# Two linear layers behind a state attention, one core: leaky ReLU on ScalarE, conversion paced by VectorE's time, turned state reads, earlier loads in the tail

## The chip, the core and the metric

The kernel runs on one core of one Trainium2 chip. Its engines have queues of their own and wait for each other by semaphores: TensorE (PE, with a queue PEld for weight loads), VectorE (DVE), ScalarE (ACT), GpSimd (POOL), and SyncE (SP), which here issues nearly all DMAs. The metric is the device time of one execution in microseconds.

## What is computed

```python
def _attn_ref(x, state):                  # x: 8 x 8 x 512 x 64, state: 8 x 8 x 32 x 64
    scores = scale * np.matmul(x, state.transpose(0, 1, 3, 2))
    ...                                   # softmax over the 32 states
    xread = np.matmul(a, state)
    scores2 = scale * np.matmul(state, x.transpose(0, 1, 3, 2))
    ...                                   # softmax over the 512 tokens
    sread = np.matmul(a2, x)
    return np.concatenate([xread, sread], axis=2)

def _moe_ref(x, w_in, w_out):             # 4352 x 512 -> 2048 -> 512
    h = x @ w_in
    g = np.maximum(0.01 * h, h)
    return g @ w_out

def _moe2_ref(x, w_gate, w_val, w_out):   # 512 -> 1536 -> 512
    g = x @ w_gate
    silu = g * (1.0 / (1.0 + np.exp(-g)))
    return silu * (x @ w_val) @ w_out
```

The weights come as 64-bit floats and are rounded to 32 bits by the kernel itself.

## The kernel before

**Numbers as high and low parts.** A product of two 32-bit matrices is made of three matmuls (`passes`): each operand is split into a high part, a cast on ACT (`split_h`, L162), and a low part, a subtraction on DVE (`split_l`, L165). Matmuls of the split parts move up to 512 columns each.

**Layer 1.** There are eight blocks of 512 tokens and, as a ninth, the tail: the 256 rows that the state reads make. `N1` = 128 slots run in one loop, 16 for each block; a slot `i` takes one of the 16 groups of 128 hidden columns. In it, `h_mm` makes the hidden values of the slot two ahead (6 matmuls into `ps_h`), `h_act` applies the leaky ReLU (an ACT copy from PSUM, L515, and a DVE operation, L516) and splits the result into `gh` and `gl`, and `y_mm` adds the slot's share to the block's output (12 matmuls into `ps_y`). In the last block (slots 112 to 127) each slot also does the tail's share (`h_mm(B, ...)`, `y_mm(B, ...)`, 256 columns, with weights `tail_in` that are split into `ch` and `cl`). The attention's steps (`read_state`, `read_tokens`) are put into slots beforehand by `put`, which keeps the sum of their DVE costs in a slot under `BUDGET`. `read_tokens` ends in `read` (16 products of 128x32 weights `et` and 64 moving columns `xn`, L400) and `read_out` (8 transposes of 32x32 from PSUM on DVE, L413).

**The conversion in the background.** Layer 2's weights have to be rounded and split before layer 2 can start. `convert` is a generator over 36 pieces ("keys") of w_gate, w_val and w_out: each key is loaded from DRAM into one of three buffers `ws`, and takes two operations on ACT (`scale`, `low`) and four on DVE (`limit` L216, `sign` L213, `join` L219, `add` L222). `finish2` is a second generator that takes finished keys in pairs, makes sums and splits of them (`hl`) and stores them in DRAM (`quad_...`, `w2_...`, `wo_...`). `pump(n)` advances the first by n steps, `pump_finish(n)` the second; a key's work is four steps. In blocks 1 to 6 a slot calls `pump(1)` once, and once more in each fourth slot; the same holds for `pump_finish`. In the last block's slots there are seven `pump(1)` and a `pump_finish(5)`. In slot `Y_SUMS` = 6 of the last block, whatever is left of both generators is run down on the spot (the drain); then its memory is handed over to the pool `wpool`, 16 places for layer 2's weights, and the first of these are loaded (`load_w`, `wq`), as are the inputs (`yr`) of `y_sums`, sums and splits of finished blocks that layer 2 starts from (`yc`, `T`).

**Order.** The program text sets the order on each engine (`manual_schedule`): an instruction that waits holds up all that stand behind it on its engine. SP issues DMAs in text order as well, with at most eight under way.

**Layer 2** goes over four pairs of blocks: products by `quads` (`ps_x`, `ps_s`, `ps_a`; L708), then `read_out(p)`, 24 steps of 12 matmuls with w_out (`ps_o`, `wo`). A step's end frees a place for the `wo` load four steps on (`load_wo`, L806). Before the last pair comes the tail: twelve steps `f`, each `hidden(f)` (24 matmuls of 256 columns into `ps_t`, with split gate and val weights `wh`, `wl`) and 6 matmuls into `ps_o`. The tail's first six generator steps run between the steps of `read_out(2)`: the first loads, the splits of `y`, and the splits of gate and val for `f` = 0 and 1. `split2` splits a loaded weight `wraw` and calls `load2` for the next load in the fixed order gate, val, o of f = 0, 1, 2 and so on. Three loads are made ahead.

Of the kernel before, what the change touches and what calls it, by code (L numbers as in the profile page):

```python
# [25 lines left out]
def kernel(  # L26
# [38 lines left out]
    nc = tc.nc  # L65
# [47 lines left out]
    Y_SUMS = 6  # L113
# [4 lines left out]
    PUMPS = [1, 1, 1, 1, 1, 1, 1]  # L118
    BUDGET = 2.8
    EARLY = -5  # L120
    BUDGET0 = 2.6
# [39 lines left out]
    def split_h(dst, src):  # L161
        nc.scalar.copy(dst, src)  # L162
# [68 lines left out]
    def convert(keys, room, prepare, load_next, finish=None):  # L231

        done, before, prev = None, None, None
        for key in keys + [None, None]:
            while key and not room(key):
                yield 0
            ops = None
# [9 lines left out]
            yield 1  # L247
# [3 lines left out]
            yield 1  # L251
            if prev:
                prev["join"]()
            yield 1
# [9 lines left out]
            yield 1  # L264
# [9 lines left out]
    def pump_finish(n):  # L274
        for _ in range(n):
            next(finishing[0], None)
# [84 lines left out]
    def read_tokens(b, q):  # L361
# [32 lines left out]
        def read():  # L394

            ps = v["ps"] = ps_a.tile([P, 512], F32, tag="b", name="ps_r")
            tokens = [xn.pop((b, p)) for p in pairs]
            for c in range(NC):
                for j in range(4):
                    nc.tensor.matmul(  # L400
                        ps[NS * j:NS * (j + 1), 0:D],
                        lhsT=v["et"][:, c * P + NS * j:c * P + NS * (j + 1)],
                        rhs=tokens[j // 2][:, c, D * (j % 2):D * (j % 2 + 1)],
                        start=(c == 0),
                        stop=(c == NC - 1),
                    )
            next_xn(2)

        def read_out():
            for j in range(4):  # L410
                for g in range(2):
                    d0 = D * (j % 2) + 32 * g
                    nc.vector.transpose(  # L413
                        out=x_tail[d0:d0 + 32, pairs[j // 2], b * NS:(b + 1) * NS],
                        in_=v["ps"][NS * j:NS * (j + 1), 32 * g:32 * g + 32],
                    )
# [6 lines left out]
            {"D": [read_out], "cost": 0.9},  # L423
# [82 lines left out]
    def h_act(j, f):  # L506
# [8 lines left out]
        nc.scalar.copy(hs, ps[:, :n])  # L515
        nc.vector.scalar_tensor_tensor(out=hs, in0=hs, scalar=0.01, in1=hs, op0=ALU.mult, op1=ALU.max)  # L516
# [174 lines left out]
    def layer2(p2, ps2):  # L691
# [167 lines left out]
        def tail():  # L859
            n = widths[B]  # L860
            order = [(key, f) for f in range(NF2) for key in ("gate", "val", "o")]
            loads = iter(order)
            raw2, parts2 = {}, {}

            def load2():
                key = next(loads, None)
                if not key:
                    return
                kind, f = key
                if kind == "o":  # L870
# [5 lines left out]
                    parts2[key] = (h, l), (ht, lt)  # L876
                else:
                    raw2[key] = wtiles[0].take("wraw")
                    nc.sync.dma_start(out=raw2[key][0], in_=w2_dram[kind, f % HF][:, f // HF])
# [7 lines left out]
            for _ in range(3):  # L887
                load2()
# [11 lines left out]
            def split2(kind, f):  # L900
                if f < NF2:
                    if kind != "o":
                        t, tag = raw2.pop((kind, f))
                        h, ht = wtiles[0].take("wh", dtype=F32R)
                        l, lt = wtiles[0].take("wl", dtype=F32R)
                        split_h(h, t)
                        split_l(l, t, h)
                        wtiles[0].give(tag)
                        parts2[kind, f] = (h, l), (ht, lt)
                    load2()  # L910
# [27 lines left out]
            split2("o", 0)  # L938
            yield
            hidden(0)  # L940
            for f in range(NF2):
                split2("gate", f + 2)
                split2("val", f + 2)
                split2("o", f + 1)
# [12 lines left out]
                wtiles[0].give(*tags)  # L957
                if f + 2 >= NF2:
# [494 lines left out]
```

## Time and profile before

| | |
|---|---|
| median of 3 runs | 1517.83 us (1517.43 to 1518.1) |
| profiled execution | 1516.83 us |
| its span, first to last instruction | 1515.0 us |
| PE busy | 1460.5 us, 96% |
| DVE busy | 944.6 us, 62% |
| ACT busy | 683.4 us, 45% |
| mean granted clock of TensorE | 0.984 |

The windows give busy times of each engine in a stretch of the span; the timeline gives single instructions with the idle time ahead of them and what ended it; the chain of waits is followed back from the last instruction. The granted clock of 1.00 is TensorE's upper level, 2.4 GHz, and 0.50 its lower one, 1.2 GHz; a mean between them is a stretch with both. Durations of matmuls are longer than the distance of their starts, because they are pipelined, so distances are used here.

### The profile page before, as it was taken

Reading aid. Unit: us, or ns where it says so; the run is one execution under the profiler, and the core shown is the slowest. Engines: PE = TensorE matmul, PEld = TensorE weight load, DVE = VectorE, ACT = ScalarE, POOL = GpSimd, SP = SyncE. Lnnn points to the kernel's source line nnn. Section 1 sums busy time; section 2 is a strip of 40 time slices with the busy share of each in tenths; the row PEclk is TensorE's granted clock in tenths of the full one; section 3 lists DMA queues with packets and bytes.
Section 4 is the critical chain, followed back from the end, with each engine's and each line's share of the span. In section 5 each row is a group of like instructions: output and inputs, shape, how many; then the busy total and the mean of one; then the engine's idle time right before and its main releaser. Section 6 shows DMA issues by size and latency. Waiting matters only on the chain.

```text
span 1515.0 us, 20085 instructions
## 1 busy us (share of the span) xinstructions
PE 1460.5 (96%) x7114; PEld 1157.6 (76%) x7114; DVE 944.6 (62%) x1716; ACT 683.4 (45%) x1234; POOL 3.0 (0%) x8
## 2 busy tenths in 40 slices
PE   6999999999999999919999999999999998999999
PEld 2446777777777788818888888888888887988887
DVE  6888688887887876976444544445344554544442
ACT  6777555565555555645433333334333342433322
POOL 0000000000000000000000000000000000000000
PEclk9999999999999999959999999999999998999999
DMA  8885444444454545785568677676766387786445
GB/s 296 294 282 198 140 157 177 153 174 157 164 194 161 188 137 183 262 271 183 162 193 274 205 235 229 194 221 228 235 200 194 105 285 230 225 279 192 130 141 193
DMA packets 146164, 307.53 MB, mean 203 GB/s; under 512 B 14608, under 2 KB 35088, under 8 KB 145040
## 3 DMA queue, kind: packets, MB, share of 16 engines
q1 hardware_dynamic: 144912, 297.85, 60.1%
q10 hardware_dynamic: 1152, 8.39, 1.3%
q8 instruction: 57, 0.93, 0.3%
q14 instruction: 43, 0.35, 0.1%
HBM read 231.74 MB, written 74.45 MB: 202 GB/s over the span
## 4 chain that ended last, share of the span: by engine, by line
PE 51%; DMA 4%; DVE 3%; ACT 1%; issue 0%; SPq 0%; ACTq 0%; DVEq 0%
PE ps_x L708 17%; PE ps_o L433 17%; PE ps_s L708 9%; PE ps_a L708 4%; DMA wraw<-w_val 2%; PE ps_y L433 1%; PE ps_h L433 1%; DMA ws<-in_dram 1%; PE ps_yt L433 1%; DMA wo<-wo 1%; PE ps_t L433 0%; DVE wl L165 0%; ACT wh L162 0%; DVE two L219 0%; DVE hl L165 0%
## 5 line engine op out<-in xcount | busy, mean ns | idle before, releaser
L433 PE MATMUL ps_y<-gh,w_parts 128*128 128x512 f32 x1024 | 339.0, 391 | 0.0
L708 PE MATMUL ps_x<-yc,wq 128*128 128x512 f32 x1152 | 278.0, 389 | 0.0
L708 PEld LDWEIGHTS ps_x<-yc,wq 128*128 128x128 f32 x1152 | 216.2, 188 | 44.8
L433 PE MATMUL ps_o<-wo,zh 128*128 128x512 f32 x768 | 236.5, 389 | 0.0
L433 PEld LDWEIGHTS ps_y<-gh,w_parts 128*128 128x128 f32 x1024 | 192.4, 188 | 52.0 <-issue 8.1
L433 PE MATMUL ps_y<-gl,w_parts 128*128 128x512 f32 x512 | 199.5, 390 | 0.2 <-DVE gl L165 0.2
L433 PEld LDWEIGHTS ps_o<-wo,zh 128*128 128x128 f32 x768 | 144.2, 188 | 30.0
L433 PE MATMUL ps_o<-wo,zl 128*128 128x512 f32 x384 | 149.5, 389 | 0.5 <-DMA wo<-wo 0.5
L708 PE MATMUL ps_s<-yc,wq 128*128 128x512 f32 x576 | 146.1, 389 | 0.0
L162 ACT CAST gh<-hs 128x512 fp32r<-128x512 f32 (+1 forms) x144 | 85.9, 596 | 118.1 <-DVE hs L516 118.1
L165 DVE TENSOR_TENSOR zl<-z,zh 128x512 fp32r<-128x512 f32 x96 | 66.3, 691 | 116.0 <-ACT zh L162 116.0
L165 DVE TENSOR_TENSOR gl<-hs,gh 128x512 fp32r<-128x512 f32 (+1 forms) x144 | 95.3, 662 | 56.9 <-ACT gh L162 54.0
L708 PEld LDWEIGHTS ps_s<-yc,wq 128*128 128x128 f32 x576 | 108.1, 188 | 22.4
L162 ACT CAST zh<-z 128x512 fp32r<-128x512 f32 x96 | 59.3, 622 | 142.1 <-PE ps_o L433 142.0
L728 ACT ACTIVATE sg<-C 128x512 f32<-128x512 f32 x72 | 45.5, 632 | 158.5 <-DVE C L724 158.5
L433 PEld LDWEIGHTS ps_y<-gl,w_parts 128*128 128x128 f32 x512 | 96.2, 188 | 20.1 <-DVE gl L165 0.5
L724 DVE TENSOR_TENSOR C<-ps_s,C 128x512 f32<-128x512 f32 x48 | 33.2, 691 | 124.2 <-PE ps_s L708 124.2
L516 DVE SCALAR_TENSOR_TENSOR hs<-hs 128x512 f32<-128x512 f32 (+1 forms) x144 | 94.5, 656 | 25.9 <-ACT hs L515 24.8
L515 ACT COPY hs<-ps_h 128x512 f32<-128x512 f32 (+1 forms) x144 | 80.5, 559 | 60.3 <-PE ps_h L433 58.5
L433 PE MATMUL ps_h<-ah,swl 128*128 128x512 f32 x256 | 106.4, 416 | 0.5 <-DVE swl L165 0.5
L433 PE MATMUL ps_h<-al,swh 128*128 128x512 f32 x256 | 100.6, 393 | 0.0
L433 PE MATMUL ps_h<-ah,swh 128*128 128x512 f32 x256 | 100.4, 392 | 0.0
(126 smaller groups left out, 2009.3 us busy)
## 6 DMA issues: line engine op xcount, KB each, us to landing
wo<-wo SPq DMA_DIRECT2D x96, 512.0 KB, 4.7
wq<-quad_gate SPq DMA_DIRECT2D x168, 256.0 KB, 3.1
wq<-quad_val SPq DMA_DIRECT2D x168, 256.0 KB, 3.1
ws<-in_dram SPq DMA_DIRECT2D x68, 512.0 KB, 4.6
sw_dram<-sw SPq DMA_DIRECT2D x56, 256.0 KB, 3.1
sw<-sw_dram SPq DMA_DIRECT2D x56, 256.0 KB, 3.8
quad_gate<-hl SPq DMA_DIRECT2D x24, 512.0 KB, 3.5
quad_val<-hl SPq DMA_DIRECT2D x24, 512.0 KB, 3.4
```

The costliest lines, as they stand in the source:

```text
L162: nc.scalar.copy(dst, src)
L165: nc.vector.tensor_tensor(out=dst, in0=src, in1=hi.bitcast(F32), op=ALU.subtract)
L433: nc.tensor.matmul(ps, lhsT=w, rhs=v, start=first and n == 0, stop=last and n == len(todo) - 1)
L515: nc.scalar.copy(hs, ps[:, :n])
L516: nc.vector.scalar_tensor_tensor(out=hs, in0=hs, scalar=0.01, in1=hs, op0=ALU.mult, op1=ALU.max)
L708: nc.tensor.matmul(bank, lhsT=a, rhs=v, start=first and n == 0, stop=last and n == len(todo) - 1, skip_group_check=True,)
L724: nc.vector.tensor_tensor(out=kept[0], in0=bank, in1=kept[0], op=ALU.add)
L728: nc.scalar.activation(t[0], c, AF.Sigmoid)
```

## The change

- The leaky ReLU is one ACT activation (Prelu) from PSUM instead of an ACT copy and a DVE operation.
- The generators' steps yield a cost in us of DVE's time. `fill(us)` runs both until the given time is used up. In blocks 1 to 6 a slot is given what is left of `SLOT` after `CHUNK` and the attention's steps, at most `FILL`, half of it ahead of `y_mm` and half behind. `pump` remains for block 0.
- In the last block each slot ahead of `Y_SUMS`, now 5, gets `fill(2.0)`. The sums' steps then run at a bounded pace, with the rest behind the loop.
- A state read is turned: `xn` (128x64) are the weights, 32 columns of `et` move, two products at a time lie in PSUM side by side, and one DVE copy takes the place of 8 transposes. Its cost for `put` is 0.2 instead of 0.9.
- In the tail's first step gate and val of f = 0 and 1 are loaded and both parts of w_out for both (8 loads instead of 4), and later loads are made two steps ahead.

```diff
-    Y_SUMS = 6
+    Y_SUMS = 5
...
-    PUMPS = [1, 1, 1, 1, 1, 1, 1]
+    BUDGET0 = 2.6
+    FILL = 1.9
+    CHUNK = 0.8
+    SLOT = 4.1
...
             if prev:
                 prev["limit"]()
-            yield 1
+            yield 0.42
             if key:
                 ops["low"]()
                 ops["sign"]()
-            yield 1
+            yield 0.42
             if prev:
                 prev["join"]()
-            yield 1
+            yield 0.69
...
-    def pump_finish(n):
-        for _ in range(n):
-            next(finishing[0], None)
+    credit = [0.0]
+
+    def fill(us):
+
+        credit[0] = min(credit[0] + us, 2.0)
+        while credit[0] > 0:
+            cost = (next(finishing[0], None) or 0) + (next(background[0], None) or 0)
+            if not cost:
+                break
+            credit[0] -= cost
...
-            ps = v["ps"] = ps_a.tile([P, 512], F32, tag="b", name="ps_r")
+            ps = v["ps"] = ps_a.tile([P, 2, NS], F32, tag="b", name="ps_r")
             tokens = [xn.pop((b, p)) for p in pairs]
-            for c in range(NC):
-                for j in range(4):
-                    nc.tensor.matmul(
-                        ps[NS * j:NS * (j + 1), 0:D],
-                        lhsT=v["et"][:, c * P + NS * j:c * P + NS * (j + 1)],
-                        rhs=tokens[j // 2][:, c, D * (j % 2):D * (j % 2 + 1)],
...
+            for i in range(2):
+                for c in range(NC):
+                    for e in range(2):
+                        n = c * P + NS * (2 * i + e)
+                        nc.tensor.matmul(
+                            ps[D * e:D * (e + 1), i],
+                            lhsT=tokens[i][:, c, D * e:D * (e + 1)],
+                            rhs=v["et"][:, n:n + NS],
...
+            nc.vector.tensor_copy(out=x_tail[:, pairs[0]:pairs[0] + 2, b * NS:(b + 1) * NS], in_=v["ps"])
...
-        nc.scalar.copy(hs, ps[:, :n])
-        nc.vector.scalar_tensor_tensor(out=hs, in0=hs, scalar=0.01, in1=hs, op0=ALU.mult, op1=ALU.max)
+        nc.scalar.activation(hs, ps[:, :n], AF.Prelu, alpha=0.01)
...
-            for _ in range(3):
-                load2()
+            for f in range(2):
+                for kind in ("gate", "val"):
+                    load2(kind, f)
+            for f in range(2):
+                load2("o", f)
...
+                    load2(kind, f + 2)
...
                 wtiles[0].give(*tags)
+                load2("o", f + 2)
...
-                pump(PUMPS[0])
+                room = min(FILL, SLOT - CHUNK - load.get(i, 0))
+                fill(room / 2)
                 next(parts)
-                pump_finish(1)
                 y_mm(j, f)
-                pump(f % 4 == 2)
-                pump_finish(f % 4 == 0)
+                fill(room / 2)
...
                 if f < Y_SUMS:
-                    pump_finish(5)
+                    fill(2.0)
                 elif f == Y_SUMS:
-                    while next(background[0], None) is not None or next(finishing[0], None) is not None:
-                        pump(1)
-                        pump_finish(1)
+                    drain()
...
-                    for _ in range(2):
+
+                    while summed[0] < min(2 * (f - Y_SUMS), f):
                         next(sums0, None)
+                        summed[0] += 1
```

DVE's queue in the last block, at the slot of the drain; a row is a line, an operation, and what it writes and reads (`two<-ws,two` as ISA is a key's `add`). Before:

```order
L165 TENSOR_TENSOR gl<-hs,gh 128x512
L213 TENSOR_SCALAR two<-ws 128x512
L219 SCALAR_TENSOR_TENSOR two<-ws,two 128x512
L222 ISA two<-ws,two 128x1024
L165 TENSOR_TENSOR hl<-two,hl 128x512 x2
L216 TENSOR_SCALAR ws<-ws 128x512
L213 TENSOR_SCALAR two<-ws 128x512
L219 SCALAR_TENSOR_TENSOR two<-ws,two 128x512
L222 ISA two<-ws,two 128x1024
```

Now, around the same slot and the one after it:

```order
L168 TENSOR_TENSOR gl<-hs,gh 128x256
L168 TENSOR_TENSOR gl<-hs,gh 128x512
L168 TENSOR_TENSOR cl<-tail_in,ch 128x512
L168 TENSOR_TENSOR gl<-hs,gh 128x256
L168 TENSOR_TENSOR gl<-hs,gh 128x512
L168 TENSOR_TENSOR swl<-sw,swh 128x512
L168 TENSOR_TENSOR cl<-tail_in,ch 128x512
L168 TENSOR_TENSOR gl<-hs,gh 128x256
L168 TENSOR_TENSOR gl<-hs,gh 128x512
L623 TENSOR_TENSOR T<-yr 128x512
```

Before, ten `add` stand between this `gl` and the next `cl`; now the 36th and last `add` stands behind 112 `gl`, ahead of the rows shown.

SP's queue in `read_out(2)`, where the tail's first loads stand between the `wo` loads. Before:

```order
L806 DMA wo<-wo_136 128x1024
L884 DMA yr<-y_dram_103 128x512 x2
L879 DMA wraw<-w_gate_108 128x512
L879 DMA wraw<-w_val_114 128x512
L875 DMA wh<-wo_132 128x512
L875 DMA wl<-wo_132 128x512
L806 DMA wo<-wo_133 128x1024
```

Now:

```order
L815 DMA wo<-wo_136 128x1024
L889 DMA yr<-y_dram_103 128x512 x2
L884 DMA wraw<-w_gate_108 128x512
L884 DMA wraw<-w_val_114 128x512
L884 DMA wraw<-w_gate_109 128x512
L884 DMA wraw<-w_val_115 128x512
L880 DMA wh<-wo_132 128x512
L880 DMA wl<-wo_132 128x512
L880 DMA wh<-wo_132 128x512
L880 DMA wl<-wo_132 128x512
L815 DMA wo<-wo_133 128x1024
```

Four more loads of 256 KB stand ahead of the third `wo` load of this read-out. On PE the order is the same in both kernels but for the form of the state reads.

## Rows read from the trace of the kernel before

**Rows 1.** The page: span; busy us of the engines, share of the span, instructions.
```profile
span 1515.0 us, 20085 instructions
...
PE 1460.5 (96%) x7114; PEld 1157.6 (76%) x7114; DVE 944.6 (62%) x1716; ACT 683.4 (45%) x1234; POOL 3.0 (0%) x8
```
**Rows 2.** Windows: stretch, length, busy of PE, PEld, DVE, ACT, POOL, clock, DMA, GB/s.
```profile
150.00:640.00 490.00, 489.71 (x2717) 393.74 (x2716) 394.49 (x810) 273.43 (x506) 0.53 (x1) 1.00 0.50 172
640.00:690.00 50.00, 17.92 (x91) 15.70 (x91) 35.46 (x66) 24.85 (x46) 0.00 (x0) 0.66 0.84 272
```
**Rows 3.** Timeline of PE, last block: start, us, line, form, [idle before, releaser].
```profile
644.54 0.28 PE L433 MATMUL ps_yt<-gh,w_parts 128*128 128x256 f32 x1
676.90 0.55 PE L433 MATMUL ps_h<-tailh,cl 128*128 128x256 f32 x1 [32.08 <-DVE cl L165]
```
**Rows 4.** Chain of waits in order of time: start, us, what; last block.
```profile
676.90 5.46 PE ps_h L433 x18
...
686.55 2.83 PE ps_h L433 x18
```
**Rows 5.** Groups by line and form, DVE, 230 to 545 us: busy, mean ns, idle before.
```profile
L516 DVE SCALAR_TENSOR_TENSOR hs<-hs 128x512 f32<-128x512 f32 x70 | 47.9, 684 | 6.9 <-ACT hs L515 6.6
...
L413 DVE STREAM_TRANSPOSE x_tail<-ps_r 32x32 f32<-32x32 f32 x98 | 20.8, 213 | 1.4
...
L222 DVE CUSTOM_DVE_ANT_0 two<-ws,two 128x1024 uint16<-128x1024 uint16 x15 | 10.3, 684 | 0.0
```
**Rows 6.** Groups by line and form, ACT reading PSUM, whole span.
```profile
L515 ACT COPY hs<-ps_h 128x512 f32<-128x512 f32 x128 | 74.7, 583 | 55.7 <-PE ps_h L433 54.0 <-ACT yst L556 1.2
...
L728 ACT ACTIVATE sg<-ps_x 128x512 f32<-128x512 f32 x24 | 14.3, 597 | 24.7 <-PE ps_x L708 24.7
```
**Rows 7.** Timeline of PE, block 0.
```profile
59.20 0.50 PE L433 MATMUL ps_h<-ah,swl 128*128 128x512 f32 x1 [0.54 <-DVE swl L165]
```
**Rows 8.** Timeline of PE, one state read in block 3.
```profile
325.51 0.39 PE L433 MATMUL ps_y<-gh,w_parts 128*128 128x512 f32 x1
325.83 0.65 PE L400 MATMUL ps_r<-xn,et 128*32 128x64 f32 x32
326.41 0.50 PE L433 MATMUL ps_h<-ah,swl 128*128 128x512 f32 x1
```
**Rows 9.** Groups by line and form, weight loads (PEld), 150 to 590 us.
```profile
L433 PEld LDWEIGHTS ps_y<-gh,w_parts 128*128 128x128 f32 x786 | 147.5, 188 | 31.4 <-ACT yst L556 0.5
...
L400 PEld LDWEIGHTS ps_r<-xn,et 128*32 128x32 f32 x512 | 7.9, 109 | 5.8 <-issue 2.1 <-ACT ws L212 1.1 <-ACT gh L162 0.7
```
**Rows 10.** Timeline of SP's queue in the third read-out.
```profile
1213.61 13.85 SPq L806 DMA_DIRECT2D wo<-wo  x6
```
**Rows 11.** Timeline of PE in the third read-out.
```profile
1221.39 0.47 PE L433 MATMUL ps_o<-wo,zl 128*128 128x512 f32 x1 [0.51 <-DMA wo<-wo]
```
**Rows 12.** Windows of 2 us in the third read-out, columns as in rows 2.
```profile
1216.00:1218.00 2.00, 2.00 (x11) 1.65 (x10) 1.29 (x2) 0.62 (x2) 0.00 (x0) 1.00 1.05 400
...
1222.00:1224.00 2.00, 2.00 (x10) 1.61 (x9) 0.86 (x2) 0.06 (x1) 0.00 (x0) 1.00 0.72 244
```
**Rows 13.** Timeline of PE in the tail of layer 2.
```profile
1270.47 0.28 PE L433 MATMUL ps_t<-yt,wl 128*128 128x256 f32 x1
...
1275.60 0.39 PE L433 MATMUL ps_t<-yt,wl 128*128 128x256 f32 x1 [1.89 <-DVE wl L165]
...
1281.12 0.58 PE L433 MATMUL ps_t<-yt,wl 128*128 128x256 f32 x1 [3.04 <-DVE wl L165]
...
1293.55 0.40 PE L433 MATMUL ps_o<-wh,zl 128*128 128x512 f32 x1
...
1297.81 0.40 PE L433 MATMUL ps_o<-wh,zl 128*128 128x512 f32 x1
...
1331.62 1.52 PE L708 MATMUL ps_x<-yc,wq 128*128 128x512 f32 x6
```
**Rows 14.** A window of 2 us in the tail, columns as in rows 2.
```profile
1276.00:1278.00 2.00, 2.00 (x11) 1.79 (x10) 0.00 (x0) 0.00 (x0) 0.00 (x0) 0.54 0.96 248
```

More of the change, by code (lines that the diff above doesn't have):

```diff
@@ L233, in convert @@
         done, before, prev = None, None, None
-        for key in keys + [None, None]:
-            while key and not room(key):
+        todo = list(keys)
+        while todo or before or (finish and done):
+            key = todo.pop(0) if todo and room(todo[0]) else None
+            if not (key or before or (finish and done)):
                 yield 0
+                continue
             ops = None
@@ L263, in convert @@
                     store(before)
-            yield 1
+            yield 0.69
             done, before, prev = before, key, ops
@@ L394, in read @@
         def read():
-            ps = v["ps"] = ps_a.tile([P, 512], F32, tag="b", name="ps_r")
+            ps = v["ps"] = ps_a.tile([P, 2, NS], F32, tag="b", name="ps_r")
             tokens = [xn.pop((b, p)) for p in pairs]
-            for c in range(NC):
-                for j in range(4):
-                    nc.tensor.matmul(
-                        ps[NS * j:NS * (j + 1), 0:D],
-                        lhsT=v["et"][:, c * P + NS * j:c * P + NS * (j + 1)],
-                        rhs=tokens[j // 2][:, c, D * (j % 2):D * (j % 2 + 1)],
-                        start=(c == 0),
-                        stop=(c == NC - 1),
-                    )
+            for i in range(2):
[6 more added lines that the diff above has]
+                            rhs=v["et"][:, n:n + NS],
+                            start=(c == 0),
+                            stop=(c == NC - 1),
+                        )
             next_xn(2)
         def read_out():
[L410 to L416, printed above, removed]
+            nc.vector.tensor_copy(out=x_tail[:, pairs[0]:pairs[0] + 2, b * NS:(b + 1) * NS], in_=v["ps"])
         return [
@@ L422, in read_tokens @@
             {"P": [read]},
-            {"D": [read_out], "cost": 0.9},
+            {"D": [read_out], "cost": 0.2},
         ]
@@ L860, in tail, with load2 @@
             n = widths[B]
-            order = [(key, f) for f in range(NF2) for key in ("gate", "val", "o")]
-            loads = iter(order)
             raw2, parts2 = {}, {}
-            def load2():
-                key = next(loads, None)
-                if not key:
+            def load2(kind, f):
+                if f >= NF2:
                     return
-                kind, f = key
                 if kind == "o":
@@ L875, in load2 @@
                         nc.sync.dma_start(out=t.bitcast(F32), in_=wo_dram[f // 2][:, f % 2, m])
-                    parts2[key] = (h, l), (ht, lt)
+                    parts2[kind, f] = (h, l), (ht, lt)
                 else:
-                    raw2[key] = wtiles[0].take("wraw")
-                    nc.sync.dma_start(out=raw2[key][0], in_=w2_dram[kind, f % HF][:, f // HF])
+                    raw2[kind, f] = wtiles[0].take("wraw")
+                    nc.sync.dma_start(out=raw2[kind, f][0], in_=w2_dram[kind, f % HF][:, f // HF])
             yr = []
@@ L901, in split2 @@
                 if f < NF2:
[L902 to L910, printed above, removed]
+                    t, tag = raw2.pop((kind, f))
+                    h, ht = wtiles[0].take("wh", dtype=F32R)
+                    l, lt = wtiles[0].take("wl", dtype=F32R)
+                    split_h(h, t)
+                    split_l(l, t, h)
+                    wtiles[0].give(tag)
+                    parts2[kind, f] = (h, l), (ht, lt)
+                    load2(kind, f + 2)
             def hidden(f):
@@ L1083, in finish2 @@
                 sums(one[:, 1, 1], one[:, 0, 1], a[:, 0])
-                yield 1
+                yield 0.84
                 sums(two[:, 0, 1], a[:, 0], a[:, 2])
@@ L1274, in take0, with drain @@
             return t, None
+        summed = [0]
         preparing, after = ExitStack(), ExitStack()
+        def drain():
+            while True:
+                steps = [next(g[0], None) for g in (finishing, background)]
+                if steps == [None, None]:
+                    return
         turn_over = max(before["state"][-1], before["tokens"][-1]) + 1
@@ L1365 @@
                     next(parts)
-                    pump(PUMPS[3])
                     next(parts)
```

22 lines of the change are left out of this document (7 added, 15 removed).

## The prediction

> **What bounds the kernel now.** I read the page's busy shares first: TensorE (PE) is busy for 1460.5 of 1515.0 us [rows 1]. So only two things can move the time: PE's idle stretches, with the slow clock that follows them, and the work that PE itself does. The windows then show where PE is idle. From 150 to 640 us it is busy for 489.71 of 490 us at a granted clock of 1.00, while VectorE (DVE) is busy for 394.49 and ScalarE (ACT) for 273.43 [rows 2]. Taking work from DVE or ACT there gives nothing by itself. From 640 to 690 us PE works for 17.92 us at a mean clock of 0.66 [rows 2]. The timeline has that stretch as one gap: the last matmul of a slot starts at 644.54, the next at 676.90, with 32.08 us of idle time put down to DVE's `cl` [rows 3]. DVE had not been slow at `cl`: in the order of before, everything left of the weight conversion stands ahead of it in the queue (the drain at `Y_SUMS`). A second and smaller loss is the tail in layer 2: gaps of 1.89 and 3.04 us at 1275.60 and 1281.12 [rows 13], and a clock of 0.54 [rows 14].
>
> **The drain.** The change paces the conversion by DVE's time, so that more of it fits into each slot of blocks 1 to 6. The order of after shows where it ends: the 36th and last join-and-add (`two<-ws,two`) stands after 112 `gl` splits on DVE, in the first slots of the last block, and `drain()` at slot 5 of that block finds nothing left. In before, ten of the 36 were left for it. What goes is the gap, 32.1 us, and the slow clock behind it: 18 matmuls that take 2.83 us when warm took 5.46 us after the gap [rows 4], so 2.6 us more. Together **-34.7**.
>
> What is late next? The conversion's work is not gone: it moves under matmuls in blocks 1 to 6, with its DMAs. Per slot (about 4.5 us there) DVE gives up one leaky ReLU of 0.684 us (70 in that window) and about 0.30 us of transposes (98 in 70 slots at 0.213) [rows 5]. It takes on 36 keys in 96 slots instead of 15 in 70, 0.16 a slot more at 2.2 us each (two operations at 0.42, two at 0.69, as the yields in the diff have them), 0.36 us, and some 0.16 us of sums and splits. DVE comes out about 0.4 us per slot lower than now, from 81% [rows 2] to some 71%. ACT gains two casts and two conversions more often and stays below 65%. The mean DMA share there is 0.50 [rows 2], and the extra traffic (about 50 GB/s on 172) makes it some 0.65. So I take 0 for the cover. If it failed, each 0.1 us per slot would cost 9.6 us.
>
> SP gets 16 `wq` loads and four `yr` loads one slot earlier. Queued behind them are the `tail_in` loads, which have three slots of lead, so 0. The last three steps of the sums now run after the loop. DVE has no `gl` left to do there, and the first products need none of their results: 0.
>
> **Prelu.** One ACTIVATE from PSUM replaces ACT's copy and DVE's operation. No row shows Prelu. Its nearest row is the Sigmoid from PSUM, 597 ns, against 583 for the copy that it replaces [rows 6]. The order has two ACT_TABLE_LOAD in both kernels, so no switch of tables is added. PE waits for neither engine in blocks 1 to 6. Only block 0 shows gaps of PE from them, 0.54 us at 59.20 [rows 7] and smaller ones. I take **-0.5**, with bounds of -1.5 and +1.
>
> **State reads.** PE's order changes nowhere else. Sixteen reads, each of 32 matmul records in 0.58 us (325.83 to 326.41) [rows 8], turn from 32 columns of weights and 64 moving to 64 of weights and 32 moving, and from four column groups side by side to two. Columns streamed per group stay equal (8 records of 64 before, 16 of 32 now), which by itself gives 0. But every record also loads its weights. LDWEIGHTS takes 109 ns for 32 columns and 188 for 128 [rows 9], so 0.82 ns a column, 53 ns for 64 above a constant part. Sixteen of these per group are 0.84 us. Against some 0.49 us now, that is +0.36 us per read (the 0.58 holds a switch between types of about 0.1 us, which stays: the matmul ahead of the read starts 0.32 us before it, where 512 columns take some 0.23 [rows 4, 8]), and all of it is on PE's path: **+5.8** for sixteen. The bounds are 0 (loads hidden) and +19 (loads of the two groups one after the other, 32 x 53 ns = 1.70 us, +1.2 each). The lower bound is nearer to the row, since 32 loads of 32 columns one after the other would already take 0.84 us and the whole read takes 0.58.
>
> The Trainium skill (TensorE: Matmul & The Clock Gate, section "Wait — 56ns, not 53.3ns?") says that matmuls never start less than about 25 ns apart, however few columns move. Here 32 start within 0.58 us [rows 8], 18 ns apart, so the floor doesn't hold across column groups in this trace. If it held for the turned form, a read would take 0.8 us and the sum would be +3.5 instead of +5.8.
>
> **Tail.** It runs from 1270.47 (first `ps_t`) to 1331.62 (first `ps_x` after it), 61.15 us; a step that waits for nothing takes 1297.81 - 1293.55 = 4.26 us, and twelve are 51.1 [rows 13]. The loss is 10.0. Now gate and val of step 1 are loaded in the first step of the tail, some 58 us before they are wanted, and each later pair two steps ahead instead of one. Both gaps go, and with them the slow clock. Step 2's val is still queued behind a `wo` load and four stores: I leave 1 us. **-9.0**, with bounds of -9.9 and -5.
>
> **The price of loading sooner.** Four more loads (1.05 MB) stand on SP's queue ahead of the third `wo` load of that read-out, as the order shows. That transfer is already the late one: issued at 1213.61 [rows 10], it made PE wait 0.51 us at 1221.39 [rows 11], and the DMA engines were full then (share 1.05, 400 GB/s) [rows 12]. 1.05 MB at 400 GB/s is +2.6 us of gap. After 0.51 us the clock stayed at 1.00 [rows 12]; after the gap of 1.89 us it fell to 0.54 [rows 13, 14]. A gap of 3.1 us is nearer to the second, so I add the 2.6 us of rows 4: **+5.2**, with bounds of 0 and +6.
>
> **Sum.** -32.1 - 2.6 - 0.5 + 5.8 - 9.0 + 5.2 = -33.2 us. The profiled execution took 1516.83 us (span 1515.0), so 1483.6. The median of the three runs is 1.0 above it: **1484.6 us**.
>
> **Rivals.**
> 1. Cheap turn, no new stall: the reads cost nothing and the `wo` load is not late. Then 1517.8 - 34.7 - 0.5 - 9.5 = 1473, or 1476 with the 2.6 us of gap. For it: equal columns per group, and loads that overlap now. Against it: the DMA share of 1.05 and the slope of LDWEIGHTS. 23%.
> 2. Dear turn: weight loads one after the other, +19 instead of +5.8, gives 1498. Against it: the 0.58 us of now. 11%.
> 3. The pace isn't kept on the chip: a `ws` load lands late, ACT (in order) waits for it, and slots in blocks 1 to 6 stretch a little, or some of the gap stays. At 0.1 to 0.25 us per slot, or a third of the gap, 1494 to 1508. For it: in the drain ACT waits for `ws` again and again. Against it: a key now has about 2.7 slots (12 us), and three buffers. 8%.
> 4. Slower than before: DVE or ACT becomes the bound in blocks 1 to 6, through `gl`, which now stands between two helpings of conversion. The helpings may fill a slot up to 4.1 us by the code's costs, and PE's bare slot (18 matmuls of 512 columns) is about as long. From 0.35 us per slot on, 96 slots eat the whole gain: 0.45 would give 1528. Against it: back-to-back operations of DVE overlap, their costs are the longer, single durations, and `gl` has two slots until its matmuls. The Trainium skill (ScalarE: Activation LUTs, section "Rules for kernel authors") speaks for this side: it wants relu and max on VectorE and not on ScalarE. Here ACT does one operation either way, of 583 or about 597 ns [rows 6]. 4%.
>
> **How the numbers follow.** Forecast, 1479 to 1491: 54%. The likeliest case gives 1484.6. With rival 1 and the lower part of rival 2, the range of 1475 to 1495 should hold 8 in 10. What a measurement of this kernel can tell from no change is about 0.2% (3 us): faster by more 0.95, within it 0.01, slower 0.04.
>
> **What the profile after would show.** Right: no gap of PE between 560 and 720 us, and no clock below 1.00 there; the first `ps_x` of layer 2 some 29 us earlier than now; the tail about 52 us long; a gap of about 3 us at the `wo` load in the third read-out, with a clock of 0.5 behind it; reads of 0.9 to 1.0 us; DVE near 71% in blocks 1 to 6. Wrong: PE waiting for `gl`, `hs` or `swl` between 150 and 560 us (rivals 3 and 4), reads of 0.58 us or of 1.8 (rivals 1 and 2), or no wait for `wo` (rival 1).

## The result and the profile after

The changed kernel takes 1483.06 us, the median of four runs (1482.04 to 1485.71), against 1517.63 for the kernel before on the same chip (1514.11 to 1518.1). The ratio is 0.978, with a 95% interval of 0.976 to 0.980. The prediction was 1484.6. The profiled execution took 1485.71 us, its span 1483.9, so the two profiles differ by 31.1 us where the medians differ by 34.6.

First the page: span, busy us of the engines, and TensorE's granted clock in 40 slices.

```profile
span 1483.9 us, 19781 instructions
...
PE 1462.7 (99%) x7114; PEld 1162.4 (78%) x7114; DVE 829.7 (56%) x1460; ACT 685.7 (46%) x1234; POOL 3.0 (0%) x8
...
PEclk9999999999999999999999999999999999999999
```

PE's busy time is nearly that of before [rows 1]; what has gone is idle time. The windows that answer to rows 2, with one more for blocks 1 to 6 (stretch, length, busy PE, PEld, DVE, ACT, POOL, clock, DMA share, GB/s):

```profile
150.00:640.00 490.00, 490.00 (x2676) 396.19 (x2675) 321.33 (x630) 290.49 (x532) 0.53 (x1) 1.00 0.58 196
640.00:690.00 50.00, 50.00 (x300) 44.73 (x300) 21.65 (x37) 24.67 (x48) 0.00 (x0) 1.00 0.37 123
150.00:560.00 410.00, 410.00 (x2245) 326.63 (x2244) 285.89 (x570) 248.97 (x453) 0.01 (x1) 1.00 0.60 207
```

The stretch from 640 to 690 us, where PE worked for 17.92 us [rows 2], is full, at a clock of 1.00. DVE stands at 70% in blocks 1 to 6 (285.89 of 410) and the DMA share at 0.60: more conversion, and PE never waits for it. The timeline of PE has these rows for a state read, layer 2's start, the third read-out and the tail:

```profile
558.74 1.12 PE L416 MATMUL ps_r<-et,xn 128*64 128x32 f32 x32
559.79 0.50 PE L443 MATMUL ps_h<-ah,swl 128*128 128x512 f32 x1
...
701.97 1.32 PE L717 MATMUL ps_x<-yc,wq 128*128 128x512 f32 x5
...
1194.82 0.77 PE L443 MATMUL ps_o<-wo,zl 128*128 128x512 f32 x1 [3.06 <-DMA wo<-wo]
...
1246.58 0.28 PE L443 MATMUL ps_t<-yt,wl 128*128 128x256 f32 x1
...
1257.18 0.39 PE L443 MATMUL ps_t<-yt,wl 128*128 128x256 f32 x1 [1.66 <-DVE wl L168]
...
1300.51 0.85 PE L717 MATMUL ps_x<-yc,wq 128*128 128x512 f32 x3
```

A read lasts 1.05 us (558.74 to 559.79), against 0.58 [rows 8]. The wait for `wo` is 3.06 us, against 0.51 [rows 11]. The tail is 53.93 us long (1246.58 to 1300.51), against 61.15, and one gap is left of two [rows 13].

To place the time I cut PE's timeline of every kernel at five marks: the first `ps_h`; the first matmul into `ps_yt` (the last block's first slot); the first `ps_x`; the first `ps_t`; the first `ps_x` after that. What follows the last mark, up to the end of the span, is 183.4 us in all of them. Each row is one profiled execution. Lengths in us:

```
                 start   blocks   last block,   layer 2       tail
                         0 to 6   sums          to the tail
before           34.37   559.55   137.17        539.38        61.15
after            33.56   565.98   102.43        544.61        53.93
difference       -0.81    +6.43   -34.74         +5.23        -7.22   = -31.1
```

### The profile page after: what moved, and what is told of

It reads as the page before. It is cut to its first block, busy times and chain, and to the rows that moved or that the text cites. A ratio compares the mean times of both kernels' runs of the same rounds, so it can differ in the third digit from the quotient of the medians.

```text
span 1483.9 us, 19781 instructions
## 1 busy us (share of the span) xinstructions
PE 1462.7 (99%) x7114; PEld 1162.4 (78%) x7114; DVE 829.7 (56%) x1460; ACT 685.7 (46%) x1234; POOL 3.0 (0%) x8
## 4 chain that ended last, share of the span: by engine, by line
PE 98%; ACT 1%; DMA 1%; DVE 1%; issue 0%; SPq 0%; ACTq 0%; DVEq 0%
PE ps_y L443 24%; PE ps_o L443 19%; PE ps_x L717 18%; PE ps_h L443 14%; PE ps_s L717 9%; PE ps_a L717 4%; PE ps_sw L456 4%; PE ps_t L443 2%; PE ps_yt L443 2%; PE ps_s L319 1%; PE ps_r L416 1%; PE ps_a L402 0%; DMA wo<-wo 0%; DMA flat<-in_dram 0%; ACT states L1205 0%
## 5 line engine op out<-in xcount | busy, mean ns | idle before, releaser
L525 ACT ACTIVATE hs<-ps_h 128x512 f32<-128x512 f32 (+1 forms) x144 | 82.7, 575 | 178.0 <-PE ps_h L443 176.8
L729 ACT COPY C<-ps_x 128x512 f32<-128x512 f32 x96 | 56.1, 584 | 94.0 <-PE ps_x L717 94.0
L443 PEld LDWEIGHTS ps_o<-wo,zl 128*128 128x128 f32 x384 | 72.8, 190 | 18.6 <-issue 3.5
```

The costliest lines, as they stand in the source:

```text
L443: nc.tensor.matmul(ps, lhsT=w, rhs=v, start=first and n == 0, stop=last and n == len(todo) - 1)
L525: nc.scalar.activation(hs, ps[:, :n], AF.Prelu, alpha=0.01)
L729: nc.scalar.copy(t[0], src)
```

## The experiments

The theory is the prediction's: the pace is worth the whole drain and needs no cover; the reads and the third `wo` load pay some of it back; the tail gains; Prelu alone is worth little. Against it stand two rivals: that VectorE's relief through Prelu makes the gain, or that VectorE's fuller queue costs something in blocks 1 to 6. The kernels ran in three groups, each with the kernel before on its chip, so I compare ratios to before and the lengths of stages. A ratio of 0.001 is 1.5 us. After has the ratio 0.978.

```
                 ratio (95%)              start  blocks  last    layer 2  tail
old_pace         0.9992 (0.9983-1.0002)   33.10  565.45  132.40  543.88   54.31
prelu_only       0.9968 (0.9956-0.9980)   32.68  557.97  134.01  539.33   62.73
no_prelu         0.9825 (0.9808-0.9843)   32.73  571.25  102.42  542.78   55.44
pace_only        0.9856 (0.9836-0.9876)   33.41  573.30  102.42  539.37   60.78
partial_drain    0.9886 (0.9871-0.9902)   32.88  565.24  116.50  543.42   53.88
old_reads        0.9741 (0.9725-0.9757)   33.24  558.23  102.43  543.34   52.97
four_groups      0.9755 (0.9742-0.9769)   32.11  560.81  102.43  542.00   53.90
o_later          0.9758 (0.9745-0.9771)   33.22  565.76  102.43  540.82   54.23
old_tail         0.9820 (0.9807-0.9834)   33.85  565.32  102.42  539.56   63.10
best             0.9708 (0.9688-0.9728)   33.47  557.77  102.42  539.03   54.05
best2            0.9700 (0.9680-0.9721)   34.38  557.68  102.43  538.58   56.33
```

### The old pace in the new kernel (old_pace)

```diff
-                room = min(FILL, SLOT - CHUNK - load.get(i, 0))
-                fill(room / 2)
+                pump(1)
                 next(parts)
+                pump_finish(1)
                 y_mm(j, f)
-                fill(room / 2)
+                pump(f % 4 == 2)
+                pump_finish(f % 4 == 0)
```

The last block's pumps, `Y_SUMS` and the order inside `convert` go back as well.

> The changed kernel with the pace of the conversion as before (fixed counts of steps per slot, ten of 36 keys left to the drain in slot 6 of the last block); Prelu, turned reads and the tail stay changed. Theory (the pace is the whole gain): the gap of 32.1 us and 2.6 us of slow clock come back, so the time is that of before plus the two losses and minus the tail's gain: 1517.6 + 7.5 (reads) + 5.3 (third wo load) - 7.2 (tail) - 0.5 = about 1522.7 us, range 1518 to 1526. Rival (the relief of VectorE by Prelu, 0.684 us per slot, is a good part of the gain): the drain itself is shorter or the slots shorter, 1485 to 1510 us.

Measured: 1514.86 us, as fast as before. Without the pace the other parts together are worth nothing, so the pace is needed for the gain. But the theory gave 1522.7 where before is 1517.6, so 5 us more than before, and the measured time is 0.9 us less than before on its chip (1515.75): 6 us are missing, and the range was missed. The stages say where: the last block with the sums takes 132.40 us, 4.8 less than before, and blocks 0 to 6 take 5.9 more where the reads alone should have cost 7.5.

### Prelu alone (prelu_only)

```diff
-        nc.scalar.copy(hs, ps[:, :n])
-        nc.vector.scalar_tensor_tensor(out=hs, in0=hs, scalar=0.01, in1=hs, op0=ALU.mult, op1=ALU.max)
+        nc.scalar.activation(hs, ps[:, :n], AF.Prelu, alpha=0.01)
```

> The kernel before with Prelu alone. Theory: nothing waits for VectorE outside the drain, so 1516 to 1518 us (-1.5 to +1 against 1517.6), the gap at cl still 30 to 32 us. Rival (VectorE's 684 ns per slot is what the gain comes from): 1507 us or less, a gap below 25 us.

Measured: 1510.85 us against 1515.75, 4.9 us less: more than the theory allowed, and less than the rival wanted. Between the two profiles blocks 0 to 6 give 1.6 of it and the last block 3.2; the start and the tail differ by 1.7 and 1.6 us in opposite directions. Three rows of the last block show how. The timeline of DVE, with the last `gl` ahead of the drain and the `cl` behind it:

```profile
631.75 0.69 DVE L165 TENSOR_TENSOR gl<-hs,gh 128x512 fp32r<-128x512 f32 x1 [0.45 <-ACT gh L162]
...
669.27 0.69 DVE L165 TENSOR_TENSOR cl<-tail_in,ch 128x512 fp32r<-128x512 f32 x1
```

And PE's gap in the same kernel:

```profile
670.10 0.55 PE L433 MATMUL ps_h<-tailh,cl 128*128 128x256 f32 x1 [28.54 <-DVE cl L165]
```

The timeline of DVE in the kernel before has the same two rows:

```profile
639.50 0.69 DVE L165 TENSOR_TENSOR gl<-hs,gh 128x512 fp32r<-128x512 f32 x1
...
676.07 0.69 DVE L165 TENSOR_TENSOR cl<-tail_in,ch 128x512 fp32r<-128x512 f32 x1
```

From `gl` to `cl`, the ten keys take 36.6 us before and 37.5 with Prelu, so the drain itself is no shorter. It begins earlier: `gl` stands 45.6 us behind the first `ps_yt` matmul (593.92) before, and 41.1 behind it (590.65) with Prelu, while the matmuls that don't need `cl` keep PE busy for 50.9 us in both. So 9.8 us of the drain lie under matmuls instead of 5.3. DVE ran behind in the last block of before: its `gl` shows no idle time ahead of it there, while with Prelu it waits 0.45 us for ScalarE's `gh`. The same earlier start is in old_pace, where PE's gap is 4.6 us shorter than before:

```profile
676.95 0.55 PE L443 MATMUL ps_h<-tailh,cl 128*128 128x256 f32 x1 [27.49 <-DVE cl L168]
```

### Some keys left to the drain (partial_drain)

```diff
-    FILL = 1.9
+    FILL = 1.5
```

> The changed kernel with FILL = 1.5 instead of 1.9: the conversion runs slower, and six of the 36 keys still stand at the drain. Theory (each key left costs TensorE what it takes in the drain, 32.1 us for ten keys, 3.2 us a key, and the slow clock 2.6 us once): +19 to +22 us, 1502 to 1505. Rival (the first keys of a drain are covered by work that is queued ahead): three or more of the six cost nothing, +12 us or less, 1495 or less.

Measured: 1498.86 us. The ratio is 0.0106 above that of after, 16 us, between the two theories; the stage is 14.1 us longer. The timeline of DVE around the drain, and then PE's gap:

```profile
632.24 0.69 DVE L168 TENSOR_TENSOR gl<-hs,gh 128x512 fp32r<-128x512 f32 x1 [1.39 <-ACT gh L165]
...
652.46 0.68 DVE L168 TENSOR_TENSOR cl<-tail_in,ch 128x512 fp32r<-128x512 f32 x1
```

```profile
653.29 0.55 PE L443 MATMUL ps_h<-tailh,cl 128*128 128x256 f32 x1 [11.24 <-DVE cl L168]
```

Six keys take 20.2 us from `gl` to `cl`, 3.4 each; ten took 37.5 and 36.6, 3.7 each. Of each such drain the first 9.8 us lie under matmuls (20.2 - 9.8 = 10.4, and 37.5 - 9.8 = 27.7; the gaps, 11.24 and 28.54, each hold 0.8 us more, from the start of `cl` to PE's). So a key costs PE some 3.5 us (an estimate, the mean of the two), and the first two or three cost nothing. The 3.2 us a key from the first on was a line through one point. VectorE isn't the only one that sets the 3.5 us: ScalarE waits for the load of a `ws` at key after key (its timeline):

```profile
638.33 0.66 ACT L214 ACTIVATE ws<-ws 128x512 f32<-128x512 f32 x1 [3.53 <-DMA ws<-in_dram]
642.34 0.67 ACT L214 ACTIVATE ws<-ws 128x512 f32<-128x512 f32 x1 [2.28 <-DMA ws<-in_dram]
```

### The change without Prelu (no_prelu)

The edit of prelu_only, undone in the changed kernel.

> The changed kernel with the leaky ReLU as before (copy on ScalarE, then an operation on VectorE), all else changed. VectorE's share from 150 to 560 us rises from 70% to about 84%. Theory (cover: VectorE's queue has slack for gl, two slots of lead): 0 to +3 us, 1483 to 1486. Rival (VectorE in order, with gl between two helpings of conversion, becomes the bound at this share): TensorE waits for gl in blocks 1 to 6, 0.1 us a slot are 9.6 us, so 1493 us or more.

Measured: 1489.79 us, between the theory's range and the rival's, at a ratio 0.0045 above after's, 6.8 us. Blocks 0 to 6 are 5.3 us longer. VectorE is at 83% (338.93 of 410) in the windows:

```profile
150.00:560.00 410.00, 407.74 (x2201) 324.48 (x2200) 338.93 (x655) 246.44 (x451) 0.00 (x0) 1.00 0.59 204
526.00:528.00 2.00, 1.70 (x6) 1.37 (x7) 1.90 (x5) 1.70 (x4) 0.00 (x0) 0.78 0.44 179
528.00:530.00 2.00, 2.00 (x6) 1.63 (x5) 1.93 (x4) 0.87 (x2) 0.00 (x0) 0.50 0.86 152
```

It is not `gl` that PE waits for, but the copy of a finished block out of PSUM (`yst`), and that copy is late because ScalarE waited for VectorE in the slots before it. The timeline of PE, then of ScalarE:

```profile
526.30 0.50 PE L443 MATMUL ps_y<-gh,w_parts 128*128 128x512 f32 x1 [2.27 <-ACT yst L566]
```

```profile
519.25 0.62 ACT L165 CAST gh<-hs 128x512 fp32r<-128x512 f32 x1 [1.66 <-DVE hs L526]
520.82 0.58 ACT L525 COPY hs<-ps_h 128x512 f32<-128x512 f32 x1
523.56 0.62 ACT L165 CAST gh<-hs 128x512 fp32r<-128x512 f32 x1 [2.16 <-DVE hs L526]
525.66 2.04 ACT L566 COPY yst<-ps_y 128x512 f32<-128x512 f32 x4
```

`gh` needs `hs`, which VectorE makes behind whatever conversion stands ahead of it in its queue. ScalarE works in order, so the four `yst` copies, and the PSUM banks that they free, come 2.3 us late; the clock falls to 0.50 behind the gap. The gap and the slow clock are some 4 of the 5.3 us (an estimate: 2.27 us, and half of the 3.4 us at 0.50); where the rest is lost is not shown. With Prelu, `hs` is ScalarE's own, and in the timeline of after the same place reads:

```profile
519.92 0.60 ACT L525 ACTIVATE hs<-ps_h 128x512 f32<-128x512 f32 x1 [1.06 <-PE ps_h L443]
520.55 0.62 ACT L165 CAST gh<-hs 128x512 fp32r<-128x512 f32 x1
523.56 2.06 ACT L565 COPY yst<-ps_y 128x512 f32<-128x512 f32 x4
```

### The pace alone (pace_only)

The changed kernel with the leaky ReLU, the reads and the tail of before.

> The new pace alone: the changed kernel with the leaky ReLU, the state reads and the tail's loads as before. Theory (the drain's cost is 34.7 us, and without Prelu ScalarE waits for VectorE's part of the leaky ReLU, so that the copies of a block's output come late once, as they did without Prelu, 2.3 us of gap and about 2 us of slow clock): 1516.6 - 34.7 + 4 to 6 = 1486 to 1488 us. Rival 1 (the pace alone has no such cost): 1482 us or less. Rival 2 (with the eight transposes as well, VectorE is at some 90% in blocks 1 to 6 and the late copies come at several block ends): 1492 us or more.

Measured: 1494.94 us against 1516.66, so 21.7 us less where the drain alone is worth 34.7: rival 2 here. The last block is as short as in after (102.42), but blocks 0 to 6 are 13.75 us longer than before. With the transposes as well, VectorE is at 87% (358.46 of 410). The pace was not made gentler for that: a read still counts 0.2 in the plan. The late copies come at four block ends, and in block 6 PE does wait for `gl`, here in a window and in PE's timeline:

```profile
150.00:560.00 410.00, 402.09 (x2200) 315.99 (x2199) 358.46 (x755) 239.17 (x448) 0.00 (x0) 1.00 0.58 203
```

```profile
236.74 0.50 PE L447 MATMUL ps_y<-gh,w_parts 128*128 128x512 f32 x1 [3.31 <-ACT yst L570]
...
310.58 0.50 PE L447 MATMUL ps_y<-gh,w_parts 128*128 128x512 f32 x1 [0.35 <-ACT yst L570]
...
455.52 0.50 PE L447 MATMUL ps_y<-gh,w_parts 128*128 128x512 f32 x1 [1.00 <-ACT yst L570]
...
529.18 0.50 PE L447 MATMUL ps_y<-gh,w_parts 128*128 128x512 f32 x1 [2.55 <-ACT yst L570]
...
579.85 0.50 PE L447 MATMUL ps_y<-gl,w_parts 128*128 128x512 f32 x1 [0.65 <-DVE gl L168]
```

The four gaps at `yst` are 7.2 of the 13.75 us. The rest is the clock of 0.50 behind the first of them, smaller waits, and some time that these rows don't place.

### The reads as before (old_reads)

The matmuls and the eight transposes of before; the cost in the plan stays at 0.2.

```diff
-                            lhsT=tokens[i][:, c, D * e:D * (e + 1)],
-                            rhs=v["et"][:, n:n + NS],
...
+                        lhsT=v["et"][:, c * P + NS * j:c * P + NS * (j + 1)],
+                        rhs=tokens[j // 2][:, c, D * (j % 2):D * (j % 2 + 1)],
```

> The changed kernel with the state reads as before (32 columns of weights, 64 moving, eight transposes on VectorE), their cost in the plan left at 0.2. Theory (a turned read costs TensorE 0.47 us more than an old one and its end is on the path): -7.5 us, 1475 to 1476. Rival (the eight transposes, 1.7 us of VectorE per read instead of one copy of 0.21, hold up gl now that the conversion fills the slots): TensorE waits, 1481 to 1490.

Measured: 1475.61 us, as the theory had it. Blocks 0 to 6 are 7.75 us shorter than in after, reads last 0.58 us again, and PE loses nothing to the transposes, with VectorE at 77% (314.45 of 410). PE's timeline, then the window:

```profile
551.14 0.65 PE L414 MATMUL ps_r<-xn,et 128*32 128x64 f32 x32
551.72 0.50 PE L447 MATMUL ps_h<-ah,swl 128*128 128x512 f32 x1
```

```profile
150.00:560.00 410.00, 410.00 (x2278) 324.52 (x2277) 314.45 (x688) 253.54 (x461) 0.53 (x1) 1.00 0.61 211
```

So turning the reads is the one part of the change that loses time on balance.

### Turned reads in four column groups (four_groups)

```diff
-                        nc.tensor.matmul(
-                            ps[D * e:D * (e + 1), i],
-                            lhsT=tokens[i][:, c, D * e:D * (e + 1)],
+                        for g in range(2):
+                            m = D * e + 32 * g
+                            nc.tensor.matmul(
+                                ps[m:m + 32, i],
+                                lhsT=tokens[i][:, c, m:m + 32],
...
```

> The changed kernel with each turned product cut into two of 32 columns of weights, so that a read has 64 matmul records in four column groups instead of 32 in two; the sum of columns of weights is the same, and so are the columns moved per record. Theory 1 (what the prediction's sum took: weight loads of the groups run side by side, so a read lasts as long as one group's loads): 16 records of 32 columns a group, about 0.6 us a read instead of 1.05, -7 us, 1476. Theory 2 (weight loads go one after the other over all groups, some 0.5 ns a column: 32 x 32 columns in 0.58 us before, 32 x 64 in 1.05 now): 64 x 32 columns, 1.05 to 1.2 us a read, 0 to +2 us, 1483 to 1485. Theory 3 (the Trainium skill, TensorE: Matmul & The Clock Gate, section Wait - 56ns, not 53.3ns?: starts at least 25 ns apart): 1.6 us a read, +9 us, 1492.

Measured: 1480.05 us, 4 us above theory 1's 1476; blocks 0 to 6 are 5.2 us shorter than in after. A read of 64 records takes 0.69 us in PE's timeline:

```profile
552.45 0.76 PE L418 MATMUL ps_r<-et,xn 128*32 128x32 f32 x64
553.14 0.50 PE L445 MATMUL ps_h<-ah,swl 128*128 128x512 f32 x1
```

Theory 1 is nearest for the read: the groups work side by side. Twice as many records take two thirds of the time. Theory 2 asked for 1.05 to 1.2 us, theory 3 for 1.6. The 25 ns between starts that the Trainium skill gives (TensorE: Matmul & The Clock Gate, section "Wait — 56ns, not 53.3ns?") don't hold across column groups here: 0.69 us for 64 is 10.8 ns.

### The tail's w_out loads later (o_later)

```diff
-            for f in range(2):
-                load2("o", f)
             yield
             y = []
             for k in range(2):
+                load2("o", k)
```

> The changed kernel with the tail's four w_out loads (f = 0 and 1, both parts) moved from the tail's first generator step to its second and third, behind the sums' steps; the four loads of gate and val stay in the first. Theory (the third wo load of that read-out is late because these loads stand ahead of it): four loads fewer, as many as in the kernel before, so the gap at wo falls from 3.1 us to about 0.5, the clock stays at 1.00, -5.3 us, 1478. Rival (the wo load is late for another reason, the inputs of the sums and the DMA share of 1.0): gap of 2 us or more and a clock of 0.5 remain, 1481 to 1484.

Measured: 1480.15 us. The third `wo` load comes as the theory said, with 0.30 us of wait; but a later one, behind the loads that were moved, now waits 0.86 (PE's timeline):

```profile
1192.01 0.47 PE L443 MATMUL ps_o<-wo,zl 128*128 128x512 f32 x1 [0.30 <-DMA wo<-wo]
...
1217.63 0.47 PE L443 MATMUL ps_o<-wo,zl 128*128 128x512 f32 x1 [0.86 <-DMA wo<-wo]
```

Layer 2 up to the tail is 3.8 us shorter than in after, of 5.2 that it had lost, so the time is some 2 us above the 1478 expected. The loads ahead of it are the cause of the third load's wait.

### The tail as before (old_tail)

The fixed order of loads, four of them in the first step, one step of lead.

> The changed kernel with the tail's loads as before (four in the first step, one step of lead). Theory: the gaps of 1.9 and 3.0 us and the slow clock in the tail come back (+7.2), the wo stall of 3.1 us goes (-5.3): about +2 us, 1485 (1483 to 1487), and the tail is 61 us long. Rival (the tail's loads only looked late because of the state of the transfers before them): the tail stays at 54 us, 1478.

Measured: 1489.48 us, above the expected 1483 to 1487. The stage ahead of the tail gives back 5.05 us, as expected. The tail takes 63.1 us, 9.2 more than in after where I expected 7.2; so by these stages the change of the loads is worth 4 us in all, not 2, and by the ratios (0.9820 against 0.978) 6. The gaps vary: 1.26 and 4.75 us here in PE's timeline, 1.89 and 3.04 before [rows 13].

```profile
1245.64 0.39 PE L443 MATMUL ps_t<-yt,wl 128*128 128x256 f32 x1 [1.26 <-DVE wl L168]
...
1252.09 0.58 PE L443 MATMUL ps_t<-yt,wl 128*128 128x256 f32 x1 [4.75 <-DVE wl L168]
```

### What beats both kernels (best, best2)

best is old_reads with the edit of o_later.

> The changed kernel with the state reads as before and the tail's w_out loads moved to its second and third step. Theory (the two costs are independent): 1475.6 - 2.9 (the difference of the run with the moved loads) to 3.8 (its stage alone) = 1472 to 1473 us, below both kernels. Rival (the loads collide with something else once the reads are short): 1475 us or more.

best2 spreads the tail's loads further (its edit of the tail against the changed kernel, in part; the reads are those of before):

```diff
-            for f in range(2):
-                for kind in ("gate", "val"):
-                    load2(kind, f)
-            for f in range(2):
-                load2("o", f)
+            for kind in ("gate", "val"):
+                load2(kind, 0)
             yield
             y = []
             for k in range(2):
+                for kind in ("gate", "val"):
+                    load2(kind, k + 1)
+                if k:
+                    load2("o", 0)
...
```

> As the run before it, with the tail's loads spread further: gate and val of f = 0 in the first step, those of f = 1 and 2 and w_out of f = 0 in the second and third, w_out of f = 1 behind the first splits. Theory: the wait for the third wo load falls below 0.3 us, and the gap of 0.7 to 1.9 us at the third group of hidden columns, which waits for a val load queued behind the stores, goes: 1 to 3 us less than the run before it, 1470 to 1472 us, the tail 52 us long. Rival (the later loads of f = 1 come too late for their splits): a gap at the second group of hidden columns, 1475 us or more.

Measured: 1472.62 and 1471.34 us, ratios of 0.9708 and 0.9700, both within what was expected. Both beat after (0.978); they can't be told apart from each other, so what best2 adds is not shown to gain anything. Neither has a wait for `wo` of 0.25 us or more in `read_out(2)`. In best2 the theory's mechanism failed and the rival came in part: the tail is 56.33 us long and not 52 (in an execution 3.3 us above the median of its five), because w_out of f = 1, moved behind the splits, is now the late load in PE's timeline:

```profile
1243.80 0.47 PE L447 MATMUL ps_o<-wh,zl 128*128 128x512 f32 x1 [0.34 <-DMA wh<-wo]
...
1245.12 0.47 PE L447 MATMUL ps_o<-wl,zh 128*128 128x512 f32 x1 [0.85 <-DMA wl<-wo]
```

## Why the prediction was right, and where it wasn't

**The drain: -34.7, measured -34.74** in its stage. The gap and the slow clock behind it were sized from rows 3 and 4, and nothing else is late there: no gap, a clock of 1.00, layer 2 starting 29.1 us earlier (701.97 against 731.09). One reading was off, to no harm: the last join-and-add comes not in the first slots of the last block but 15 us ahead of its first `ps_yt` matmul (599.54), as DVE's timeline has it:

```profile
584.50 0.69 DVE L225 CUSTOM_DVE_ANT_0 two<-ws,two 128x1024 uint16<-128x1024 uint16 x1
```

**The cover at 0** held in after: no wait between 150 and 640 us. But I put this down to VectorE's share of some 71% (70% measured) and to the slack of `gl`, and the reason lies elsewhere. The narrow place is the round trip from ScalarE to VectorE and back in the leaky ReLU, ahead of the `yst` copies. With it, the same pace costs 5.3 us at a share of 83% and 13.75 us at 87%. Prelu takes the round trip away, and lowers the share as well: no run has Prelu above 77%, so that the round trip decides is read from the rows of ScalarE and not shown by a run that changes it alone. The forecast priced Prelu at next to nothing and rested its 0 on the share; without Prelu that 0 would have been wrong.

**Prelu: -0.5, measured -1.6** in blocks 0 to 6, by itself. That it would have shortened the drain by 3.2 us doesn't add, since the drain is gone. Beside the new pace it is worth 5.3 us in blocks 0 to 6, 6.8 by the ratios. I priced it as an exchange of two durations, 597 for 583 ns [rows 6]; 599 is what after's groups by line and form show:

```profile
L525 ACT ACTIVATE hs<-ps_h 128x512 f32<-128x512 f32 x128 | 76.6, 599 | 131.7 <-PE ps_h L443 130.6 <-DVE r L352 0.5 <-DVE st L353 0.5
```

What I left out was the wait between the two engines. Rival 4 named `gl` as the place and 43 us as the price (1528 against 1484.6). Without Prelu its direction is right, the place is above all `yst` (in pace_only PE waits for `gl` too, 0.65 us at most), and the price 5.3 or 13.75 us. The rule of the Trainium skill that I weighed for that rival (ScalarE: Activation LUTs, section "Rules for kernel authors", relu on VectorE, which it backs with VectorE's speed in bf16) doesn't fit this queue of 32-bit values: with the operation on VectorE the time was 6.8 us longer by the ratios.

**The reads: +5.8, measured +7.5** (0.47 us more for each of sixteen), +7.75 in the stage. That the weight loads aren't hidden was right, the size a quarter too small. I let only the loads of the weights count in the turned form. The three forms fit another reading, an estimate from their rows: loads and streaming within one column group go one after the other, and the groups side by side. A group handles 8 x (32 + 64) = 768 columns in the old form, 16 x (64 + 32) = 1536 in the turned one, and 16 x (32 + 32) = 1024 in four groups. With 0.1 us off for the switch of types, 0.48, 0.95 and 0.59 us are 0.63, 0.62 and 0.58 ns a column.

**The tail: -9.0, measured -7.2** between the two profiles, and -9.2 against old_tail. I left 1 us of loss; one gap of 1.66 us and its edges left some 2.8 (53.93 - 51.1). It is the one I named, the val load of step 2 behind four stores and a `wo` load.

**The third `wo` load: +5.2, measured +5.23** in its stage, but half of that is luck. 2.6 us of gap were added (3.06 against 0.51), and in the windows the clock falls as I supposed from the two gaps of before:

```profile
1194.00:1196.00 2.00, 1.18 (x3) 1.03 (x4) 0.00 (x0) 0.00 (x0) 0.00 (x0) 0.50 1.04 401
1196.00:1198.00 2.00, 2.00 (x7) 1.54 (x6) 0.00 (x0) 0.00 (x0) 0.00 (x0) 0.50 0.42 170
1198.00:1200.00 2.00, 2.00 (x6) 1.61 (x5) 0.00 (x0) 0.00 (x0) 0.00 (x0) 0.50 0.01 2
```

In the profile of four_groups PE waits as long at the same place, and the clock stays at 1.00:

```profile
1188.27 0.47 PE L445 MATMUL ps_o<-wo,zl 128*128 128x512 f32 x1 [3.13 <-DMA wo<-wo]
```

```profile
1188.00:1190.00 2.00, 1.73 (x8) 1.46 (x9) 0.00 (x0) 0.00 (x0) 0.00 (x0) 1.00 0.98 369
```

Its stage takes 542.00 us, 2.6 more than before, and in old_reads and partial_drain, with gaps of 2.94 and 2.92 us, some 4. So the gap of the term was sized rightly, and the 2.6 us of slow clock on top came in after's profile and not in each.

**The sum: -33.2; -31.1 between the profiles and -34.6 between the medians.** The errors (-1.1 for Prelu, +1.7 for the reads, +1.8 for the tail, -0.8 for the start) partly cancel and leave +1.6 of the +2.1 between the profiles. That the median lies 1.5 us from the forecast is therefore in part luck; the drain, by far the largest term, is not. The start differs by up to 2.3 us between profiles (32.11 to 34.38), and the profiled execution of after is the longest of its four.

## What to carry to other kernels

A gap in which an engine waits for a queue that holds work put there by the program's order is worth its whole length, with the slow clock behind it, when that work is spread ahead of it. The last two or three keys need not be spread, by the rows of partial_drain: in a drain that many lie under queued matmuls. Before spreading it, look for round trips between two in-order engines: the fuller queue makes each of them longer, and the victim is whatever stands behind the waiting instruction on its engine, here a copy that frees PSUM. Loads made sooner are paid by the transfer that stands behind them: put each as late as its own consumer allows.

## What was not expected of the hardware

Three forms of a read fit an estimate in which weight loads and moving columns cost the same within a column group (0.58 to 0.63 ns a column); no fourth form tested it. In four groups 64 small matmuls start 10.8 ns apart on average. Prelu from PSUM takes 599 ns for 128x512, and the copy in its place took 583 [rows 6]. The length of a gap doesn't say by itself whether the clock falls: after a gap of 2.27 us (no_prelu) the granted clock was 0.50 for a stretch, after one of 3.13 us (four_groups) it stayed at 1.00, and so it did after one of 1.66 us (a window of after):

```profile
1258.00:1260.00 2.00, 1.93 (x13) 1.55 (x12) 1.35 (x3) 1.73 (x4) 0.00 (x0) 1.00 0.80 221
```
